# The order of dV and dK at the start of an attention backward pass

## The chip, the cores and the metric

The kernel runs on one core of one Trainium2 chip. The metric is the time of one execution on the device in microseconds (us). The kernel before took 1716.59 us, the median of 3 runs (1715.66 to 1716.76). The profile was taken from one execution whose span was 1714.6 us.

## The reference

One transformer block is computed for one decode step, and then the gradients of everything that goes in. There are 4 sequences, one token each, model width 512, 32 heads of 128, and a cache of 4096 keys and values per sequence and head, all in bf16. The part that matters here is attention:

```python
q = (x @ wq).reshape(B, Sq, H, Dh).transpose(0, 2, 1, 3)
scores = jnp.einsum("bhqd,bhkd->bhqk", q, k_cache) * (Dh ** -0.5)
p = _softmax(scores, axis=-1)
o = jnp.einsum("bhqk,bhkd->bhqd", p, v_cache)
```

A gated MLP follows. The outputs are the block's output and the gradients for x, both caches and all five weights. The gradients of the caches are the large ones. With 4 x 32 = 128 pairs of sequence and head (called heads from here on), each cache is 128 pieces of 4096 x 128 values, 1 MB each. With one query per head, both gradients are outer products: dV of a head is the column p (4096 values) times the row dO (128 values), and dK is the column dS times the row q. dO is the gradient of the attention output, and dS = p (dP - c) times the scale, with dP = V dO and c the sum of dO times O for the head. So dV needs only p and dO, while dK needs dP, for which all of V of that head has to be read again.

## The kernel before, in words

**Forward.** A loop over pairs of heads reads K and V of each head from memory once, computes scores, softmax and output, and keeps p of all heads on chip (`P_all`, 128 x 128 x 32). Then the MLP runs forward and backward, which ends with the gradient `dhT` at the output projection.

**Backward.** V of every head is read a second time, and 128 pieces of dV and 128 pieces of dK are written. For each head s:

- `load_V2` reads V of the head, issued by ACT (nine heads are read by SP ahead of the backward part). Seven slots form a ring for these loads.
- `front(s)` transposes V on TensorE in four groups of eight (`V_T`, line 764), ACT copies each group back from PSUM (line 765), and eight matmuls with the stationary `zd` (line 1178) add dP of the head into a PSUM tile that four heads share. `zd` is written by GpSimd (`dO_window`, line 1143).
- `group_dS(g)` makes dS of four heads at once on VectorE (lines 1192, 1195), after the shared dP tile was copied by ACT and transposed by TensorE.
- `grad_V(s)` and `grad_K(s)` each run one `outer` on VectorE (line 770), which writes 128 x 4096 values into a slot. dV is then stored from GpSimd's queue (line 781), dK from SP's queue (line 1202). For dV, GpSimd first writes p twice side by side (`P_pairs`, line 1148).
- `replicate(i0)` spreads rows of dO and of q over all partitions for four heads: four matmuls into the one PSUM bank of the pool `psrep`, and one copy by ACT, for `rdo` and then for `rq`. Two buffers each, used in turn.

**Order.** The order of instructions is written by hand: each engine runs its instructions in the order in which the Python code issues them, and an engine waits when something that its next instruction needs is not there. So a GpSimd copy stands behind every store that GpSimd issues before it. The loop over heads runs `front` five heads ahead of `grad_K` (L = 5) and `grad_V` three heads ahead (LV = 3):

```python
for s in range(NH):
    load_ahead(s + L)
    if s % REP == 0 and s + REP < NH:
        replicate(s + REP)
    P_pairs(s + L)
    if s + L < NH:
        front(s + L)
    ...
    if s > 0 and s + LV < NH:
        grad_V(s + LV)
    grad_K(s)
```

Ahead of it five heads of `front` are run, with dV of heads 2 and 3. dV of heads 0 and 1 comes earlier still, at the end of the MLP part, from rows of dO made there.

**Slots.** 23 slots of a little over 1 MB hold what is read and written. A list `free` is used first in, first out: `Slot(...)` takes the first, `give()` puts a slot at the end. A slot is given back in the code as soon as the store from it has been issued. Whoever takes it next waits until that store has landed. Slots of the output weights come free page by page, those of the first two V heads go to `free` too. Slots of dV of heads 0 and 1 are held back in `first_gv` and given back only after `front(0)` and `front(1)`.

**Side work.** In the loop `step("o")` prepares dO of later heads from step 2 on (one unit per head), and `step("s")` makes the gradients of the weights and of x from step 21 on: one unit per head, three from head 59.

Of the kernel before, what the change touches and what calls it, by code (L numbers as in the profile page):

```python
# [9 lines left out]
FP32 = mybir.dt.float32  # L10
# [14 lines left out]
def kernel(  # L25
# [22 lines left out]
    nc = tc.nc  # L48
    P = nc.NUM_PARTITIONS
# [5 lines left out]
    Dh = A_k_cache.shape[3]  # L55
    F = B_w1.shape[1]
    NH = B * H
# [105 lines left out]
    ident_b = const.tile([P, P], BF16, name="ident_b")  # L163
# [14 lines left out]
    def ones_window(col):  # L178
# [11 lines left out]
                          in_=rowg[:, None, :, None].to_broadcast([P, 4, 8, 4]))  # L190
# [70 lines left out]
    with ExitStack() as c0:  # L261
# [19 lines left out]
        for r in range(2):  # L281
            for t_ in range(2):
                for q in range(4):
                    nc.tensor.matmul(qr_ps[32 * q:32 * (q + 1), 2 * r + t_, :], lhsT=ident_b[:, 64 * r + t_:64 * (r + 1):2],
                                     rhs=qT_bf[:], start=True, stop=True, tile_position=(0, 32 * q))
# [314 lines left out]
    def step(k, n=1):  # L600
        for _ in range(n):
            next(units[k], None)
# [114 lines left out]
    dOrows_bf = pers2.tile([NH, Dh], BF16, name="dOrows_bf")  # L717
# [4 lines left out]
    qrows_bf = pers2.tile([NH, Dh], BF16, name="qrows_bf")  # L722
# [29 lines left out]
    REP = B  # L752
    reps = {}
# [10 lines left out]
                nc.tensor.transpose(pt[:, i, :], v[:, g * GW + i, :], ident_b[:])  # L764
            nc.scalar.copy(out=v[:, g * GW:(g + 1) * GW, :], in_=pt[:])  # L765

    P2s, first_gv = {}, []

    def outer(dst, col2, row):
        nc.vector.tensor_tensor(  # L770
            out=dst.rearrange("p j (r t) -> p j r t", t=2),
            in0=col2[:, :, None, :].to_broadcast([P, SJ, Dh // 2, 2]),
            in1=row.rearrange("p (r t) -> p r t", t=2)[:, None, :, :].to_broadcast([P, SJ, Dh // 2, 2]),
            op=ALU.mult,
        )

    def grad_V(s):
        b, h = bh_of(s)
        gv = Slot("gv")
        outer(gv.heads(), P2s.pop(s), reps["rdo", s // REP][:, s % REP, :])  # L780
        nc.gpsimd.dma_start(out=rows_of(out_3[b, h]), in_=gv.heads())  # L781
        if s > 1:
            gv.give()
        else:
            first_gv.append(gv)

# [6 lines left out]
    def load_V2(eng=nc.sync):  # L793
        s = nv["next"]
        if s < NH:
            V2s[s] = Slot("V2", vring if vring else free)
            eng.dma_start(out=V2s[s].heads(), in_=cache_head(A_v_cache, s))
            nv["next"] += 1

    with ExitStack() as cm:  # L800
# [33 lines left out]
        for wi, wt in enumerate((w1, w3)):  # L834
            for fc in range(FC):
                for cc in range(DC):
                    nc.tensor.matmul(gu_ps[:, wi, fc, :], lhsT=w13_view(wt, cc)[:, fc * P:(fc + 1) * P], rhs=hhatT[:, cc, :],
                                     start=(cc == 0), stop=(cc == DC - 1))
# [25 lines left out]
        for jj in range(DC):  # L864
            i_mm = 0
            for (lt, wt) in ((d_gateT_bf, w1), (d_upT_bf, w3)):
                for fc in range(FC):
                    nc.tensor.matmul(dn_ps[:, jj, :], lhsT=w13_view(wt, jj)[:, fc * P:(fc + 1) * P], rhs=lt[:, fc, :],
                                     start=(i_mm == 0), stop=(i_mm == 2 * FC - 1))
                    i_mm += 1  # L870
        for sl in w1 + w3:
            sl.give()
        rs = Slot("reps")
        rep_bufs = {nm_: [rs.b()[:, (2 * k + i) * 512:(2 * k + i + 1) * 512].rearrange("p (i d) -> p i d", i=REP) for i in range(2)]
                    for k, nm_ in enumerate(("rq", "rdo"))}
# [4 lines left out]
        ps = psA.tile([P, REP, Dh], FP32, tag="rT", name="repq_ps")  # L880
# [4 lines left out]
        for s in range(3):  # L885
# [8 lines left out]
                         start=True, stop=True)  # L894
# [32 lines left out]
    with ExitStack() as c2:  # L927
        psT = c2.enter_context(tc.tile_pool(name="psT2", bufs=2, space=bass.MemoryType.PSUM))
        psD = c2.enter_context(tc.tile_pool(name="psD", bufs=1, space=bass.MemoryType.PSUM))
        psrep = c2.enter_context(tc.tile_pool(name="psrep", bufs=1, space=bass.MemoryType.PSUM))  # L930
# [176 lines left out]
        def rest_of_dO():  # L1107
            for pg in range(1, H // 8):
                while wo_units and wo_units[0] < 4 * (pg + 1):
                    woT_unit(psT, wo_units.popleft(), "s")  # L1110
                    yield
                dO_columns(8 * pg, 8 * pg + 8, psg, "gps")
                yield
                dO_rows(8 * pg, 8 * pg + 8, psg, "gps")
                mid_w["wo"][pg].give()
                yield
            dr_ps = psg.tile([B, D], FP32, tag="gps", name="dr_ps")
            for c in range(DC):
                nc.tensor.transpose(dr_ps[:, c * P:(c + 1) * P], dhT_f[:, c, :], ident_f[:])
            nc.scalar.copy(out=dh, in_=dr_ps[:])  # L1120

        units["o"] = rest_of_dO()
        def replicate(i0):
            K_ = 8 * B if i0 < 8 * B else P
            for nm_, rows in (("rdo", dOrows_bf), ("rq", qrows_bf)):
                if (nm_, i0 // REP) in reps:
                    continue
                ps = psrep.tile([P, REP, Dh], FP32, tag="rep", name="rep_ps")
                for i in range(REP):
                    nc.tensor.matmul(ps[:, i, :], lhsT=ident_b[0:K_, i0 + i:i0 + i + 1].to_broadcast([K_, P]), rhs=rows[0:K_, :],  # L1130
                                     start=True, stop=True)
                rt = rep_bufs[nm_][i0 // REP % 2]
                nc.scalar.copy(out=rt, in_=ps[:])  # L1133
                reps[nm_, i0 // REP] = rt

        rows = {}
        dS2s = {}
# [7 lines left out]
        def P_pairs(s):  # L1145
            if s < NH and s not in P2s:
                P2s[s] = bw3.tile([P, SJ, 2], BF16, tag="P2", name="P2")
                nc.gpsimd.tensor_copy(out=P2s[s][:], in_=P_all[:, s, :, None].to_broadcast([P, SJ, 2]))  # L1148
# [13 lines left out]
        def front(s):  # L1162
            hl = s % B
            if s not in VTs:
                for g in range(SJ // GW):
                    V_T(s, psT, range(g, g + 1))
                    if hl == 0 and g == 0:
                        rows_out()
                    if hl == 0 and g == 2:
                        rows_T()  # L1170
            VT = VTs[s].heads()
            if hl == 0:
                rows["acc"] = psD.tile([P, 512], FP32, tag="dP", name="dP_ps")
            dO_window(s)
            for u in range(2):
                for c in range(4):
                    j0 = 8 * c + 4 * u
                    nc.tensor.matmul(rows["acc"][32 * c:32 * (c + 1), :], lhsT=zq_window(zd[hl], 2 * hl + u),  # L1178
                                     rhs=VT[:, j0:j0 + 4, :], start=(hl == 0 and u == 0),
                                     stop=(hl == B - 1 and u == 1), tile_position=(0, 32 * c))  # L1180
            if hl == B - 1:
                rows["ps"] = rows.pop("acc")
            sl = VTs.pop(s)
            (vring if len(V2s) + len(VTs) + len(vring) < NV2 else free).append(sl.i)

        def group_dS(g):
            i0 = g * B
            T = rows.pop("T").rearrange("p jj (c m) -> p c m jj", c=4)
            t = rows.pop("t")[:, 0:B * SJ].rearrange("p (b j) -> p b j", b=B)
            t5 = t.rearrange("p b (c u jj) -> p b c u jj", c=4, u=2)  # L1190
            for hl in range(B):
                nc.vector.tensor_scalar(out=t5[:, hl], in0=T[:, :, 2 * hl:2 * hl + 2, :], scalar1=c_rep[:, i0 + hl:i0 + hl + 1],  # L1192
                                        scalar2=scale, op0=ALU.subtract, op1=ALU.mult)
            dS2s[g] = bw3.tile([P, B, SJ, 2], BF16, tag="dS2", name="dS2", bufs=1)
            nc.vector.tensor_tensor(out=dS2s[g][:], in0=t[:, :, :, None].to_broadcast([P, B, SJ, 2]),
                                    in1=P_all[:, i0:i0 + B, :, None].to_broadcast([P, B, SJ, 2]), op=ALU.mult)
# [10 lines left out]
                load_V2(nc.scalar)  # L1207


        O0, S0, L, LV = 2, 21, 5, 3  # L1210

        def load_ahead(s):
            prefetch()
            if s < NH and s not in V2s and s not in VTs:
                load_V2(nc.scalar)

        for s in range(L):
            load_ahead(s)
            P_pairs(s)
            front(s)  # L1220
            if s < 2:
                first_gv[s].give()
            elif s < LV + 1:
                grad_V(s)
        group_dS(0)
        for s in range(NH):
            load_ahead(s + L)
            if s % REP == 0 and s + REP < NH:
                replicate(s + REP)
            P_pairs(s + L)  # L1230
            if s + L < NH:
                front(s + L)
            elif s + L == NH:
                rows_out()
                rows_T()
            if s > 0 and s + LV < NH:
                grad_V(s + LV)
            grad_K(s)
            if s % B == B - 1 and s + 1 < NH:
                group_dS((s + 1) // B)  # L1240
            if s >= S0:
                step("s", 1 if s < S0 + 38 else 3)
            elif s >= O0:
                step("o")
# [31 lines left out]
```

## Time and profile before

| | busy us | share of the span | instructions |
|---|---|---|---|
| TensorE, matmul (PE) | 1271.0 | 74% | 16180 |
| TensorE, weight load (PEld) | 944.0 | 55% | 16180 |
| VectorE (DVE) | 1228.3 | 72% | 1293 |
| ScalarE (ACT) | 969.3 | 57% | 1502 |
| GpSimd (POOL) | 472.3 | 28% | 823 |
| DMA, mean rate | 413 GB/s | | 101740 packets, 707.49 MB |

The page cuts the span into 40 slices of about 43 us, with one digit per engine and slice for its busy share in tenths and the rate of the transfers below. The forward part fills slices 1 to 16, the backward part begins in slice 17. Rows by windows give the same for stretches of any length. A timeline lists the instructions of one engine in order of time: start, duration, engine, line, operation, what it writes and reads, how often; in square brackets the idle time of the engine just before, and what ended it. The costs of single operations in the backward part:

| operation | times | mean ns |
|---|---|---|
| `outer` of dV or dK, DVE | 256 | 2290 |
| copy of eight transposed tiles, ACT | 512 | 1024 |
| dP matmul, PE | 1024 | 453 |
| copy of rep rows, ACT | 62 | 587 |
| P copied in pairs, POOL | 127 | 1056 |
| `zd` written, POOL | 128 | 729 |

The median time from issue to landing is 28.1 us for a store of dV, 19.5 us for a store of dK and 15.6 us for a load of V.

### The profile page before, as it was taken

Reading aid. Unit: us, or ns where it says so; the run is one execution under the profiler, and the core shown is the slowest. Engines: PE = TensorE matmul, PEld = TensorE weight load, DVE = VectorE, ACT = ScalarE, POOL = GpSimd, SP = SyncE. Lnnn points to the kernel's source line nnn. Section 1 sums busy time; section 2 is a strip of 40 time slices with the busy share of each in tenths; the row PEclk is TensorE's granted clock in tenths of the full one; section 3 lists DMA queues with packets and bytes.
Section 4 is the critical chain, followed back from the end, with each engine's and each line's share of the span. In section 5 each row is a group of like instructions: output and inputs, shape, how many; then the busy total and the mean of one; then the engine's idle time right before and its main releaser. Section 6 shows DMA issues by size and latency. Waiting matters only on the chain. (4 is left out here: it accounts for less than half of the span.)

```text
span 1714.6 us, 38302 instructions
## 1 busy us (share of the span) xinstructions
PE 1271.0 (74%) x16180; PEld 944.0 (55%) x16180; DVE 1228.3 (72%) x1293; ACT 969.3 (57%) x1502; POOL 472.3 (28%) x823
## 2 busy tenths in 40 slices
PE   5889888888888888777667777774666776877760
PEld 4767776676666667554445455553454544454440
DVE  5989899989998996466666667663557456565484
ACT  3555444544544454676665655553656775776761
POOL 1211232222222221132231323132335133323250
PEclk9999999999999999998888886876878786677886
DMA  9999999999999999799999999999999999999998
GB/s 400 424 424 424 425 423 424 424 423 422 420 423 411 419 408 399 296 407 425 424 424 423 424 423 424 423 425 424 390 383 372 425 425 421 422 423 423 424 424 337
DMA packets 101740, 707.49 MB, mean 413 GB/s; under 512 B 11052, under 2 KB 15288, under 8 KB 17600
## 3 DMA queue, kind: packets, MB, share of 16 engines
q1 hardware_dynamic: 63568, 432.04, 60.5%
q0 software_dynamic: 20864, 148.22, 20.6%
q10 hardware_dynamic: 17136, 124.79, 17.7%
q8 instruction: 127, 2.08, 0.5%
q14 instruction: 45, 0.37, 0.1%
HBM read 422.59 MB, written 282.34 MB: 411 GB/s over the span
## 5 line engine op out<-in xcount | busy, mean ns | idle before, releaser
L765 ACT COPY V<-pt_tps 128x1024 bf16<-128x1024 bf16 x512 | 491.4, 1024 | 194.9 <-PE pt_tps L764 126.8
L764 PE MATMUL pt_tps<-ident_b,V 128*128 128x128 bf16 x4096 | 370.7, 254 | 144.5 <-ACT V L765 138.9
L764 PEld LDWEIGHTS <-V 128*128 128x128 bf16 x4096 | 320.1, 117 | 214.5 <-issue 206.0
L770 DVE TENSOR_TENSOR gk<-dS,reps 128x4096 bf16<-128x4096 bf16 x128 | 292.6, 2287 | 111.1 <-DMA out_dram<-gv 98.2
L770 DVE TENSOR_TENSOR gv<-P,reps 128x4096 bf16<-128x4096 bf16 x125 | 286.8, 2294 | 117.3 <-DMA out_dram<-gv 106.3
L421 DVE TENSOR_TENSOR PK<-Kn,PK 128x4096 bf16<-128x4096 bf16 x128 | 292.3, 2283 | 26.3 <-POOL PK L417 25.8
L436 PE MATMUL M_ps<-PK,Vn 128*128 128x130 bf16 x4096 | 285.1, 222 | 32.9 <-DMA Vn<-in_A_v_cache_dram 32.2
L436 PEld LDWEIGHTS <-Vn 128*128 128x128 bf16 x4096 | 252.8, 99 | 53.1 <-DMA Vn<-in_A_v_cache_dram 45.8
L328 DVE STREAM_TRANSPOSE KT<-Kn 128x512 f32<-128x512 f32 (+1 forms) x321 | 250.6, 797 | 0.3 <-issue 0.2
L1178 PE MATMUL dP_ps<-V,zd 128*32 128x512 bf16 x1024 | 180.4, 453 | 83.7 <-ACT V L765 61.7
L323 ACT COPY KT<-pt_tps 128x1024 bf16<-128x1024 bf16 x128 | 129.5, 1012 | 184.4 <-PE pt_tps L322 147.1
L781 POOL DMA_DIRECT2D out_dram<-gv x128 | 68.2, 533 | 547.8 <-DVE gv L770 525.0
L417 POOL COPY PK<-P_all 128x64 bf16<-128x64 bf16 x128 | 32.6, 255 | 414.4 <-ACT P_all L411 411.4
L334 POOL TENSOR_TENSOR W<-qrep,wmask 128x128 bf16<-128x128 bf16 x128 | 123.9, 968 | 82.4 <-PE S_ps L354 67.4
L1148 POOL COPY P<-P_all 128x64 bf16<-128x64 bf16 x127 | 134.1, 1056 | 0.0
L1178 PEld LDWEIGHTS <-zd 128*32 128x32 bf16 x1024 | 36.5, 96 | 169.9 <-issue 136.3
L1192 DVE TENSOR_SCALAR dPr<-dPT_ps,c_rep 128x32 f32<-128x32 f32 x128 | 23.1, 242 | 128.4 <-PE dPT_ps L1160 128.2
L1143 POOL COPY zd<-dOT_bf 128x2 bf16<-128x2 bf16 x128 | 93.3, 729 | 3.0 <-PE dP_ps L1178 3.0
L411 ACT COPY P_all<-pt_P 32x64 bf16<-32x64 bf16 x256 | 52.1, 203 | 53.5 <-PE pt_P L407 51.2
L322 PE MATMUL pt_tps<-ident_b,Kn 128*128 128x128 bf16 x1024 | 80.5, 223 | 0.0
L446 PE MATMUL kP_ps<-PK,onesw 128*32 128x512 bf16 x1024 | 79.2, 386 | 0.0
L1133 ACT CAST reps<-rep_ps 128x512 bf16<-128x512 f32 x62 | 36.4, 587 | 71.9 <-PE rep_ps L1130 36.3
(244 smaller groups left out, 1365.7 us busy)
## 6 DMA issues: line engine op xcount, KB each, us to landing
Kn<-in_A_k_cache_dram SPq DMA_DIRECT2D x128, 1024.0 KB, 15.3
Vn<-in_A_v_cache_dram SPq DMA_DIRECT2D x128, 1024.0 KB, 15.7
out_dram<-gv POOLq DMA_DIRECT2D x128, 1024.0 KB, 28.1
out_dram<-gk SPq DMA_DIRECT2D x128, 1024.0 KB, 19.5
V<-in_A_v_cache_dram ACTq DMA_DIRECT2D x119, 1024.0 KB, 15.6
V<-in_A_v_cache_dram SPq DMA_DIRECT2D x9, 1024.0 KB, 18.6
wq<-in_A_wq_dram SPq DMA_DIRECT2D x8, 1024.0 KB, 19.1
out_dram<-gw POOLq DMA_DIRECT2D x6, 896.0 KB, 27.8
```

Source lines behind the costliest of these rows:

```text
L322: nc.tensor.transpose(pt[:, i, :], Kn[:, c * GW + i, :], ident_b[:])
L323: nc.scalar.copy(out=KT[:, c * GW:(c + 1) * GW, :], in_=pt[:])
L328: nc.vector.transpose(out=KT[:, c * w_:(c + n) * w_], in_=Kn[:, c * w_:(c + n) * w_])
L334: nc.gpsimd.tensor_tensor(out=W[:, hl], in0=qrep[:, :, s:s + 1].to_broadcast([P, 4, 32]), in1=wmask[:, hl, None, :].to_broadcast([P, 4, 32 ...
L421: nc.vector.tensor_tensor(out=PK[:, :, 0:Dh].rearrange("p j (r t) -> p j r t", t=2), in0=Ks[s].heads().rearrange("p j (r t) -> p j r t", t=2),
L436: nc.tensor.matmul(hold["M"][:], lhsT=Vn[:, j, :], rhs=PK[:, j, :], start=(j == 0), stop=(j == SJ - 1))
L764: nc.tensor.transpose(pt[:, i, :], v[:, g * GW + i, :], ident_b[:])
L765: nc.scalar.copy(out=v[:, g * GW:(g + 1) * GW, :], in_=pt[:])
L770: nc.vector.tensor_tensor(out=dst.rearrange("p j (r t) -> p j r t", t=2), in0=col2[:, :, None, :].to_broadcast([P, SJ, Dh // 2, 2]), in1=r ...
L1143: nc.gpsimd.tensor_copy(out=zd[s % B][:, 32:132:67], in_=dOT_bf[:, s:s + 1].to_broadcast([P, 2]))
L1148: nc.gpsimd.tensor_copy(out=P2s[s][:], in_=P_all[:, s, :, None].to_broadcast([P, SJ, 2]))
L1178: nc.tensor.matmul(rows["acc"][32 * c:32 * (c + 1), :], lhsT=zq_window(zd[hl], 2 * hl + u), rhs=VT[:, j0:j0 + 4, :], start=(hl == 0 and u ...
```

## The change

dV runs ahead of dK by more heads at the start: in the lead-in, dV of heads 2 to 7 is run (two heads after each of the first three `front` calls), so that eight heads of dV are done before the first dK. The lead stays at eight and shrinks by one every four steps from step 16 on, down to three. It is meant to give the DMA engines something to store while the first dS is made. For that, dO rows and q rows are replicated on their own schedules: `rdo` two heads before dV needs it, `rq` two heads before dK needs it. `P_pairs` moves into the new function `more_V`, behind the dV that it follows. The list `first_gv` goes: the slots of dV of heads 0 and 1 are given back at once.

```diff
-    P2s, first_gv = {}, []
+    P2s = {}
...
         nc.gpsimd.dma_start(out=rows_of(out_3[b, h]), in_=gv.heads())
-        if s > 1:
-            gv.give()
-        else:
-            first_gv.append(gv)
+        gv.give()
...
-        def replicate(i0):
+        def replicate(nm_, i0):
+            if i0 >= NH or (nm_, i0 // REP) in reps:
+                return
...
-        O0, S0, L, LV = 2, 21, 5, 3
+        O0, S0, L = 2, 21, 5
+        gvd = {"n": 2}
+
+        def more_V(upto):
+            while gvd["n"] < min(NH, upto):
+                s = gvd["n"]
+                P_pairs(s)
+                replicate("rdo", s - s % REP)
+                grad_V(s)
+                P_pairs(s + 1)
+                P_pairs(s + 2)
+                gvd["n"] += 1
+                if s % REP == 2:
+                    replicate("rdo", s + 2)
+
+        def lead_V(s):
+            return 8 - min(5, max(0, s - 12) // 4)
...
+        replicate("rdo", REP)
         for s in range(L):
             load_ahead(s)
-            P_pairs(s)
             front(s)
-            if s < 2:
-                first_gv[s].give()
-            elif s < LV + 1:
-                grad_V(s)
+            more_V(min(2 * s + 4, 8))
         group_dS(0)
         for s in range(NH):
             load_ahead(s + L)
-            if s % REP == 0 and s + REP < NH:
-                replicate(s + REP)
-            P_pairs(s + L)
+            if s % REP == 2:
+                replicate("rq", s + 2)
             if s + L < NH:
                 front(s + L)
...
-            if s > 0 and s + LV < NH:
-                grad_V(s + LV)
+            if s > 0:
+                more_V(s + 1 + lead_V(s))
             grad_K(s)
```

More of the change, by code (lines that the diff above doesn't have):

```diff
@@ L1122 @@
         units["o"] = rest_of_dO()
-        def replicate(i0):
+        def replicate(nm_, i0):
+            if i0 >= NH or (nm_, i0 // REP) in reps:
+                return
             K_ = 8 * B if i0 < 8 * B else P
[L1125 to L1134, printed above, removed]
+            rows = dOrows_bf if nm_ == "rdo" else qrows_bf
+            ps = psrep.tile([P, REP, Dh], FP32, tag="rep", name="rep_ps")
+            for i in range(REP):
+                nc.tensor.matmul(ps[:, i, :], lhsT=ident_b[0:K_, i0 + i:i0 + i + 1].to_broadcast([K_, P]), rhs=rows[0:K_, :],
+                                 start=True, stop=True)
+            rt = rep_bufs[nm_][i0 // REP % 2]
+            nc.scalar.copy(out=rt, in_=ps[:])
+            reps[nm_, i0 // REP] = rt
         rows = {}
```

## The prediction

> **What bounds the kernel now.** I read the page's slices first, then the same stretch cut finer, then each engine's timeline there. On the page, the DMA engines are full almost everywhere:
>
> ```profile
> DMA  9999999999999999799999999999999999999998
> GB/s 400 424 424 424 425 423 424 424 423 422 420 423 411 419 408 399 296 407 425 424 424 423 424 423 424 423 425 424 390 383 372 425 425 421 422 423 423 424 424 337
> ```
>
> The kernel is bound by transfers at about 424 GB/s, so a 1 MB head (1,049 kB) costs 1,049/424 = 2.47 us, and time is won only where the rate falls. It falls in slice 17 (296), in slices 29 to 31 (390, 383, 372), and at the two ends. The change acts first on slice 17, where the backward part begins. The answer by windows of 5 and 10 us (busy us of PE, weight load, DVE, ACT, POOL; then granted clock, DMA share, GB/s):
>
> ```profile
> 700.00:705.00 5.00, 1.28 (x15) 0.88 (x12) 3.38 (x5) 2.07 (x3) 2.02 (x8) 1.00 0.86 357
> 705.00:710.00 5.00, 4.18 (x42) 2.96 (x43) 2.32 (x2) 2.59 (x3) 1.49 (x8) 0.66 0.53 220
> 710.00:715.00 5.00, 3.45 (x42) 2.12 (x43) 2.27 (x1) 3.72 (x5) 1.40 (x7) 1.00 0.82 333
> 715.00:720.00 5.00, 3.50 (x43) 2.17 (x43) 0.00 (x0) 3.77 (x5) 0.19 (x1) 1.00 0.57 210
> 720.00:725.00 5.00, 3.50 (x39) 2.17 (x38) 0.22 (x2) 3.72 (x6) 0.00 (x0) 1.00 0.59 211
> 725.00:730.00 5.00, 3.68 (x39) 2.37 (x39) 4.71 (x7) 3.38 (x5) 0.00 (x0) 0.92 0.46 147
> 730.00:740.00 10.00, 7.71 (x84) 5.11 (x82) 7.54 (x4) 7.35 (x9) 5.09 (x6) 0.87 0.97 379
> 740.00:750.00 10.00, 6.74 (x78) 4.26 (x75) 5.64 (x7) 8.71 (x10) 2.13 (x3) 1.00 1.01 425
> ```
>
> Against 424 these rows lack (67+204+91+214+213+277) x 5 + 45 x 10 = 5,780 kB between 700 and 740, or 13.6 us. DVE is idle there while PE and ACT prepare dK. The timeline of DVE says why:
>
> ```profile
> 698.50 2.29 DVE L770 TENSOR_TENSOR gv<-reps 128x4096 bf16<-128x4096 bf16 x1
> 701.03 2.28 DVE L770 TENSOR_TENSOR gv<-reps 128x4096 bf16<-128x4096 bf16 x1
> 706.58 2.29 DVE L770 TENSOR_TENSOR gv<-reps 128x4096 bf16<-128x4096 bf16 x1 [3.16 <-PE dP_ps L1178]
> 709.98 2.29 DVE L770 TENSOR_TENSOR gv<-P,reps 128x4096 bf16<-128x4096 bf16 x1 [1.10 <-POOL P L1148]
> 724.78 0.73 DVE L1192 TENSOR_SCALAR dPr<-dPT_ps,c_rep 128x32 f32<-128x32 f32 x4 [12.51 <-PE dPT_ps L1160]
> 726.00 2.29 DVE L770 TENSOR_TENSOR gk<-dS,reps 128x4096 bf16<-128x4096 bf16 x1
> ```
>
> Four dV heads, then 12.5 us of nothing, until five `front` calls, 5.0 us each, have given the first dS. The timelines of POOL and PE show what is queued behind the first stores:
>
> ```profile
> 701.09 0.63 POOL L781 DMA_DIRECT2D out_dram<-gv  x1 [3.82 <-DVE dOT_bf L739]
> 703.62 0.54 POOL L781 DMA_DIRECT2D out_dram<-gv  x1 [1.90 <-DVE c_rep L749]
> 705.06 0.20 POOL L1143 COPY zd<-dOT_bf 128x2 bf16<-128x2 bf16 x1
> 731.62 1.48 POOL L1148 COPY P<-P_all 128x64 bf16<-128x64 bf16 x1
> 733.04 2.26 POOL L1143 COPY zd<-dOT_bf 128x2 bf16<-128x2 bf16 x1
> ```
>
> ```profile
> 705.32 1.05 PE L1178 MATMUL dP_ps<-V,zd 128*32 128x512 bf16 x8 [3.68 <-POOL zd L1143]
> ```
>
> POOL issues the dV stores and also writes `zd`, without which PE can't do dP and, in order behind it, the transposes of the next head. The `zd` copy takes 0.20 us at 705 but 2.26 us at 733, where DVE runs an `outer` from 732.92 to 735.24.
>
> **What the Trainium skill says.** "SBUF — State Buffer", section "SBUF: two separate sides": DVE and GpSimd share a port pair under an exclusive lock, held for a whole instruction, and a DVE operation with two SBUF inputs takes it against a GpSimd operation that reads SBUF. The trace agrees (0.20 us against 2.26). The same section warns that a DVE operation in a two-port mode also keeps GpSimd from writing DMA descriptors. For this operation the trace does not show it: the store issued at 701.09 moved bytes from 702.0 on while DVE ran until 703.3. "DMA: Bandwidth & Descriptors", section "Anatomy of one DMA — SWDGE (gpsimd) path": about 2.0 us plus bytes/436e3 us, so 4.4 us for a head; the lone store issued at 709.17 landed in 4.4 us.
>
> **The change part by part.** *dV of heads 4 to 7 moves ahead of dK.* Nothing is added to DVE's or the DMA's total work: four heads of 2.29 us and 2.47 us move into the hole. If all fitted without disturbing anything, 4 x 2.47 = 9.9 us of the 13.6 would be filled.
>
> *The slot of head 0 is returned at once.* In the built program gv(0) and gv(1) now take the same slot (before, `first_gv` held slot 11 and gv(1) took slot 0). So gv(1) waits for the first store to land. It landed 5.5 us after 701.09, that is 706.6; with no second store beside it, say 706.0. gv(1) then runs 706.0 to 708.3 instead of 701.03 to 703.3. Behind it on POOL stand its store (708.6), the cast of dOT_f, the four memsets and the first `zd`. gv(2), which now has a free slot, starts at 708.5 and holds the port till 710.8, so memsets and `zd` follow at about 711.7. Behind `zd` waits PE's dP of head 0: 711.8 instead of 705.3, **6.5 us later**, and every `front` after it.
>
> *POOL's order.* After the change `zd` of head 1 stands behind the store of gv(3), and gv(3) waits for the store of gv(1): 708.6 + 4.4 = 713.0, so it runs to 715.3. The P copy ahead of `zd` then waits for gv(4) (to 717.6) and `zd` for gv(5) (to 719.9). PE would have been ready at about 716.6, so 3.3 us more are lost; the later `zd` copies come about as PE needs them. The extra rep copy in the lead-in costs 0.4 + 0.6 us. Sum for the first dS: 6.5 + 3.3 + 0.4, **10.2 us**; the first gk starts at about 736 instead of 726.
>
> *The transfers with these times.* By 740: what moved by 709 without gv(1) (1,785 + 1,098 - 1,049 = 1,834 kB), seven dV heads (7,340), the V loads of heads 9 and 10 (2,097) and 1.6 us of the next two (680): 11,950 kB = 28.2 us of 40, so 11.8 us lost against 13.6: 1.8 us won. One bound more: in the kernel before, the first gk and the V load beside it ran slowly (82, 213, 336, 221, 262 GB/s from 728 to 733, or 2.4 us lost). If that restart is as slow after the change, the gain is 1.8 - 2.4 = -0.6. I take +1.0, with both ends kept.
>
> *The lead shrinking from 8 to 3 at heads 16 to 32.* Five steps have no dV. The 20 steps hold 55 transfers instead of 60: 6.8 us a step against 7.4. `front` and a wo transpose came every 5.3 to 6.4 us (the V loads of ACT at 739.27, 744.84, 751.24), so compute still keeps up: cost nothing, hidden behind the transfers. At the end the lead is 3 as before, so the tail is unchanged.
>
> *rq and rdo replicated apart, earlier.* The same 62 copies. ACT's waits for a gk still reading the buffer (20.2 us, 7 times) and PE's for the one rep bank (35.2 us, 31 times) should go. From 730 to 1200 the DMA is full, so nothing is gained there. From 1200 to 1340 the rate fell to 385, 391, 425, 353, 405, 351, 387 in windows of 20 us, 12.8 us lost, where PE, ACT and DVE in turn run late. Four groups of heads there, perhaps 0.6 us each (the gap between the two copies is 0.5 to 0.7 us): 0 to 2.5 us, taken as 1.0. Those holes start from waits for wq and for old gk stores, which the change leaves.
>
> Sum: -1.0 - 1.0 = -2.0 us, 1714.6.
>
> **The rivals.** *The holding on POOL is milder* (copies slip in between DVE operations; dP of head 1 at 716.6): the first dS is only some 7 us late, 3.3 us more are won, the restart is overlapped by waiting dV stores and the later holes shrink by 2: 1.8 + 3.3 + 2 = 7, so 1709.5. For it: gv(5) and gv(6) each wait for a landing, which leaves DVE gaps. Against: 733.04. *The wait of gv(1) is harmless*: all 9.9 us, 1706.7. For it: the hole is wide. Against: PE stood 3.68 us for that very `zd`. *The new waits are worse*: a P copy at 1310.13 took 8.10 us under back-to-back `outer` operations. If that hits a `zd` in the lead-in, dK starts some 15 us late and V loads, issued by ACT behind each `front`, with it: 5 more us of DMA idle, less the 1 to 2 won: 1720, slower.
>
> **How the numbers follow.** Near-cancellation 0.53, milder 0.26, full gain 0.08, worse 0.13. So 1714.6; faster by over 3.4 us 0.34, within 0.53, slower 0.13. The range leaves out the full gain (0.08) and about half of the worst case: 1709.0 to 1719.0.
>
> **What would show it.** On DVE, gv(1) starting near 706 with a wait for a gv store; `zd` of head 0 near 711.7; eight gv before the first gk, which starts near 736; the rate from 700 to 740 still under 424 by about 12 us' worth; no ACT wait for gk at the rep copies. I am wrong if gv(1) starts near 701, if the first gk stays near 726 to 730, or if the holes from 1200 to 1340 change by several us.

## The result, and the profile after

The changed kernel took 1714.35 us (median of 4 runs, 1713.38 to 1718.53); the kernel before, beside it, 1716.13 us (1715.66 to 1716.76). The ratio is 0.9994, with a 95% interval of 0.9977 to 1.0011: no difference that this measurement can tell. A second measurement with more runs, told below, gave 1.0001 (0.9992 to 1.0010). Single executions of one kernel lie several us apart (13 of the changed kernel in the second measurement took 1712.39 to 1720.62 us), so spans of single profiles are not compared here to the microsecond; places within a profile are.

The profile of the changed kernel comes from an execution whose span was 1716.7 us. In it the backward part began 1.0 us later than in the profile of before (first dV, gv(0), at 699.52 us instead of 698.50), so I give moments in the lead-in as distance from gv(0). The slices of the page first:

```profile
DMA  9999999999999999799999999999999999999997
GB/s 402 424 425 424 424 423 425 424 424 424 414 423 409 420 406 399 318 397 425 424 426 425 412 424 425 426 426 425 420 365 381 421 421 408 419 422 425 423 424 312
```

Slice 17, at which the change was aimed, has 318 GB/s instead of 296, and slice 18 has 397 instead of 407. The hole is still there. A small dip is new in slice 23 (412). The same stretch by windows (busy us of PE, weight load, DVE, ACT, POOL; then granted clock, DMA share, GB/s):

```profile
700.00:705.00 5.00, 3.07 (x59) 2.57 (x56) 2.11 (x3) 3.13 (x5) 0.63 (x1) 0.84 0.91 378
705.00:710.00 5.00, 0.00 (x0) 0.00 (x0) 2.90 (x3) 0.00 (x0) 0.31 (x1) 0.50 0.14 61
710.00:715.00 5.00, 2.46 (x23) 1.62 (x24) 2.12 (x2) 0.37 (x1) 3.37 (x10) 0.50 0.81 341
715.00:720.00 5.00, 2.98 (x30) 2.06 (x29) 4.87 (x3) 3.49 (x4) 2.77 (x5) 0.74 0.57 238
720.00:725.00 5.00, 2.99 (x40) 1.98 (x39) 4.74 (x3) 3.76 (x4) 4.72 (x6) 0.94 0.96 390
725.00:730.00 5.00, 4.45 (x43) 3.17 (x40) 1.33 (x1) 3.63 (x5) 2.68 (x7) 0.72 1.00 351
730.00:740.00 10.00, 7.00 (x84) 4.57 (x83) 5.62 (x8) 7.49 (x9) 0.00 (x0) 1.00 0.98 337
740.00:750.00 10.00, 6.96 (x82) 4.30 (x81) 6.66 (x4) 7.67 (x10) 4.17 (x5) 1.00 1.00 390
```

From 720 to 730 the transfers now run at 390 and 351 GB/s, where before they ran at 211 and 147. But from 705 to 710 PE and ACT do nothing at all and the rate is 61 GB/s. From 725 to 740 the DMA share is 0.98 to 1.00 while only 337 to 351 GB/s move. The timeline of DVE:

```profile
699.52 2.29 DVE L770 TENSOR_TENSOR gv<-reps 128x4096 bf16<-128x4096 bf16 x1
707.10 2.29 DVE L770 TENSOR_TENSOR gv<-reps 128x4096 bf16<-128x4096 bf16 x1 [4.96 <-DMA out_dram<-gv]
709.41 2.28 DVE L770 TENSOR_TENSOR gv<-reps 128x4096 bf16<-128x4096 bf16 x1
714.57 11.76 DVE L770 TENSOR_TENSOR gv<-P,reps 128x4096 bf16<-128x4096 bf16 x5 [2.88 <-DMA out_dram<-gv]
734.31 0.73 DVE L1189 TENSOR_SCALAR dPr<-dPT_ps,c_rep 128x32 f32<-128x32 f32 x4 [7.98 <-PE dPT_ps L1157]
735.53 2.29 DVE L770 TENSOR_TENSOR gk<-dS,reps 128x4096 bf16<-128x4096 bf16 x1
```

Eight heads of dV stand before the first dK, as written. gv(1) waits 4.96 us for the landing of the first dV store. The idle time ahead of the first dS is 7.98 us instead of 12.51, but the first gk comes 36.0 us after gv(0) instead of 27.5. The timelines of POOL and of PE's dP show the chain between:

```profile
709.69 0.54 POOL L781 DMA_DIRECT2D out_dram<-gv  x1 [6.95 <-DVE c_rep L749]
712.30 0.19 POOL L1140 COPY zd<-dOT_bf 128x2 bf16<-128x2 bf16 x1
...
717.16 0.53 POOL L781 DMA_DIRECT2D out_dram<-gv  x1 [3.80 <-DVE gv L770]
717.69 1.47 POOL L1145 COPY P<-P_all 128x64 bf16<-128x64 bf16 x1
719.10 0.19 POOL L1140 COPY zd<-dOT_bf 128x2 bf16<-128x2 bf16 x1
```

```profile
712.54 1.04 PE L1175 MATMUL dP_ps<-V,zd 128*32 128x512 bf16 x8 [8.30 <-POOL zd L1140]
719.35 0.61 PE L1175 MATMUL dP_ps<-V,zd 128*32 128x512 bf16 x8 [1.73 <-POOL zd L1140]
724.19 1.24 PE L1175 MATMUL dP_ps<-V,zd 128*32 128x512 bf16 x8 [1.00 <-POOL zd L1140]
```

PE stands 8.30 + 1.73 + 1.00 = 11.03 us for `zd` in the lead-in, where before it stood 3.68 us once. A second profile of the same kernel has 9.59 + 1.70 + 0.28 = 11.57 us; in it gv(1) comes 8.3 us and the first gk 36.1 us after gv(0).

To compare whole runs I worked out, from windows of 20 us, how many us of full transfer each stage lacks: the sum of (424 - rate) x 20 / 424. A small negative value means that the stage ran at 425 to 426. The stages begin at the same moment in every profile; moving the first one by the 1.0 us by which the changed kernel is late gives 12.0 for it instead of 12.1.

| kernel (one profile each) | 700-760 us | 760-1180 | 1180-1360 |
|---|---|---|---|
| before | 13.5 | 0.1 | 12.8 |
| changed | 12.1 | 0.0 | 11.0 |
| changed, second profile | 12.1 | 3.7 | 3.6 |
| changed, slots of gv(0), gv(1) held back | 11.7 | -0.2 | 10.6 |
| changed, `zd` ahead of the stores | 10.8 | 2.5 | 10.0 |
| changed, both | 6.8 | 1.0 | 10.0 |
| changed, slots held, `zd` of four heads up front | 7.3 and 7.1 | 0.7 and 0.8 | 9.0 and 7.9 |
| the same, `zd` early in the loop too | 7.1 | 0.8 | 7.6 |
| changed, lead stays 8 | 12.5 | -1.6 | 8.9 |
| changed, slots held, `zd` of four heads up front, lead stays 8 | 7.2 | -1.1 | 10.0 |
| changed, lead shrinks 28 steps later | 12.0 | 5.0 | 5.5 |
| changed, lead shrinks in five steps on end | 12.2 | -1.6 | 13.7 |
| before, with rq and rdo replicated apart | 14.7 | -1.0 | 10.3 |

The first column is steady: five profiles with the changed lead-in give 12.0 to 12.5. The two other columns are not: the two profiles of the changed kernel itself have 0.0 and 11.0, and 3.7 and 3.6. So a difference of a few us there, between single profiles, says little about a kernel.

### The profile page after: what moved, and what is told of

Same layout as the page of the kernel before. It is cut to its first block, busy times and chain, and to the rows that moved or that the text cites. A ratio compares the mean times of both kernels' runs of the same rounds, so it can differ in the third digit from the quotient of the medians.

```text
span 1716.7 us, 38321 instructions
## 1 busy us (share of the span) xinstructions
PE 1252.2 (73%) x16180; PEld 930.7 (54%) x16180; DVE 1228.7 (72%) x1293; ACT 967.6 (56%) x1502; POOL 523.7 (31%) x821
## 5 line engine op out<-in xcount | busy, mean ns | idle before, releaser
L764 PE MATMUL pt_tps<-ident_b,V 128*128 128x128 bf16 x4096 | 361.4, 250 | 168.2 <-ACT V L765 162.2
L764 PEld LDWEIGHTS <-V 128*128 128x128 bf16 x4096 | 310.6, 114 | 232.4 <-issue 224.0
L1175 PE MATMUL dP_ps<-V,zd 128*32 128x512 bf16 x1024 | 172.6, 453 | 111.7 <-ACT V L765 55.9
L1145 POOL COPY P<-P_all 128x64 bf16<-128x64 bf16 x125 | 151.7, 1214 | 0.0
L1140 POOL COPY zd<-dOT_bf 128x2 bf16<-128x2 bf16 x128 | 130.3, 1022 | 0.0
L1130 ACT CAST reps<-rep_ps 128x512 bf16<-128x512 f32 x62 | 36.4, 587 | 98.4 <-PE rep_ps L1127 59.6
L411 ACT COPY P_all<-pt_P 32x64 bf16<-32x64 bf16 x256 | 52.1, 203 | 53.9 <-PE pt_P L407 51.6
## 6 DMA issues: line engine op xcount, KB each, us to landing
V<-in_A_v_cache_dram ACTq DMA_DIRECT2D x119, 1024.0 KB, 13.5
```

What stands on the lines that cost most here:

```text
L1140: nc.gpsimd.tensor_copy(out=zd[s % B][:, 32:132:67], in_=dOT_bf[:, s:s + 1].to_broadcast([P, 2]))
```

## The experiments

Each group of runs shares its runs of the kernel before, on the same chip; kernels of different groups are compared by their ratios. Medians are in us; the ratio is to the kernel before, with its 95% interval.

### The changed kernel once more

Edit: none.

> The changed kernel once more, beside the others of this set. Theory (near-cancellation): -2 us against the kernel before, 1713 to 1715.5; gv(1) starts about 5 us after the first dV store with a wait for it, first dK near 735, and 700 to 740 us lacks about 12 us' worth of transfers. Rival (the first profile of it, 1718.5, was the typical case): 1716 or more.

1714.91 beside 1714.85 (43 runs of before), ratio 1.0001 (0.9992 to 1.0010). The change as a whole is worth nothing within 0.1%. This is the value that the next experiments are read against.

### The slots of gv(0) and gv(1) held back again

```diff
-        gv.give()
+        if s > 1:
+            gv.give()
+        else:
+            first_gv.append(gv)
...
             front(s)
+            if s < 2:
+                first_gv[s].give()
             more_V(min(2 * s + 4, 8))
```

> The changed kernel, with the slots of dV of heads 0 and 1 held back again until front(0) and front(1), as before the change. Theory (the early return of the slot makes gv(1) wait for a landing, and everything behind it on GpSimd and TensorE moves 6.5 us): gv(1) back at about 701, the first zd at about 705, the first dK at about 730 to 732 (zd of heads 1 to 3 still stand behind the stores), 700 to 740 lacks about 7 us' worth instead of 12 to 14, and the time falls by 4 to 6 us against the changed kernel: about 1709.5. Rival (the slot wait is hidden, since the dV stores that follow fill the DMA anyway): first dK within 1 us, the same time within 1.5 us.

1713.37, ratio 0.9989 (0.9983 to 0.9996). gv(1) again starts 2.5 us after gv(0), and the first dP comes 6.7 us after gv(0) instead of 13.0. Yet the first gk comes 35.0 us after gv(0), 1.0 us sooner. PE's dP in this kernel, by the timeline:

```profile
706.81 1.04 PE L1178 MATMUL dP_ps<-V,zd 128*32 128x512 bf16 x8 [1.85 <-POOL zd L1143]
715.01 1.04 PE L1178 MATMUL dP_ps<-V,zd 128*32 128x512 bf16 x8 [3.40 <-POOL zd L1143]
723.69 1.04 PE L1178 MATMUL dP_ps<-V,zd 128*32 128x512 bf16 x8 [4.00 <-POOL zd L1143]
```

The wait of 8.30 us shrinks to 1.85, and those of the next heads grow from 1.73 and 1.00 to 3.40 and 4.00: 9.25 us in all against 11.03. The wait for the slot is real, but behind it stands the next one, `zd` behind dV stores on GpSimd.

### `zd` of the next head written before the dV stores

```diff
         def dO_window(s):
+            if s >= NH or s in zds:
+                return
+            zds.add(s)
...
             front(s)
+            dO_window(s + 1)
             more_V(min(2 * s + 4, 8))
```

> The changed kernel, with zd of the next head written by GpSimd right after each front call of the lead-in, ahead of the two dV stores, instead of behind them. Theory (zd of heads 1 to 3 behind the stores costs TensorE about 3 to 4 us): no wait of the dP matmuls for zd of heads 1 to 3, the first dK about 3 to 4 us earlier than in the changed kernel, the time 1 to 3 us lower, about 1712.5. Rival (this delay is hidden behind the dV stores that are moving at that time): first dK earlier, but the time within 1 us of the changed kernel.

1715.04, ratio 1.0004 (0.9996 to 1.0012). The later waits of PE for `zd` in the lead-in are gone, but the first, 8.47 us, stays, and the first gk comes 34.4 us after gv(0). In the first column 1.3 us is won, and nothing of it is seen in the time.

### Both repairs

Edit: the two diffs above together.

> Both at once: the slots of dV of heads 0 and 1 held back, and zd of the next head ahead of the stores. Theory: the two delays add, so the first dK starts at about 726 to 728, nearly as in the kernel before, the four dV heads fill 8 to 10 of the 13.6 us, 700 to 740 lacks 4 to 5 us' worth, and the time is 7 to 9 us below the changed kernel's start, about 1707. Rival (the hole is kept open by V loads, which can't start earlier than front frees their slots): no better than holding the slots alone, 1709.5 to 1711. Second rival (later holes between 1200 and 1340 grow by what is won at the start): the first dK early, the time still 1713 or more.

1710.07, ratio 0.9971 (0.9960 to 0.9982): 4.8 us under the changed kernel, where the single repairs gave 1.5 and nothing. The first gk comes 30.2 us after gv(0), and PE now stands 1.94 us for the first `zd` and 2.58 us for that of head 3:

```profile
705.11 1.04 PE L1183 MATMUL dP_ps<-V,zd 128*32 128x512 bf16 x8 [1.94 <-POOL zd L1148]
723.00 1.05 PE L1183 MATMUL dP_ps<-V,zd 128*32 128x512 bf16 x8 [2.58 <-POOL zd L1148]
```

The hole holds 6.8 us instead of 12.1; these 5.3 us fit the 4.8 us of time. The two waits cover each other: whichever is taken away alone, the other ends only a little earlier. By the times alone this is near the edge of the intervals; the hole says it clearly, with 0.4 and 1.3 us won by the single repairs and 5.3 by both. That the two delays would simply add, and give 1707, was a wrong expectation.

### `zd` of four heads up front, twice

The slots of gv(0) and gv(1) are held back here as above; `zd` of heads 0 to 3 is written ahead of the lead-in, later ones two heads ahead in it. The kernel was measured in two groups.

```diff
+        for s in range(B):
+            dO_window(s)
         for s in range(L):
             load_ahead(s)
             front(s)
+            dO_window(s + 2)
+            if s < 2:
+                first_gv[s].give()
             more_V(min(2 * s + 4, 8))
```

> The kernel that holds the first two slots, with zd of all four first heads written before any later dV store, and in the lead-in two heads ahead. Theory (zd behind stores is what still delays front(3) by 2.6 us when zd is one head ahead): no wait of the first 20 dP groups for zd, the first dK 2 to 3 us earlier against the first dV than with zd one ahead (about 27.5 us after it, as in the kernel before), 700 to 760 lacks 5 us' worth or less, the time about 1 to 2 us below the kernel with zd one ahead: 1708 to 1709. Rival (by then the DMA has dV to move and the earlier front is hidden): first dK earlier, the loss from 700 to 760 and the time as with zd one ahead, 1710.

1707.91 beside 1714.61, ratio 0.9965 (0.9952 to 0.9977). Its second measurement:

> The kernel with both repairs of the lead-in and the lead shrinking as in the changed kernel, once more beside the one that keeps lead 8. Theory A: ratio 0.9965 as before, so 2 to 4 us slower than the one with lead 8. Theory B: the same time as the one with lead 8.

1708.42 beside 1714.97, ratio 0.9962 (0.9950 to 0.9974). The timeline of DVE in this second profile:

```profile
698.39 2.29 DVE L770 TENSOR_TENSOR gv<-reps 128x4096 bf16<-128x4096 bf16 x1
700.92 2.28 DVE L770 TENSOR_TENSOR gv<-reps 128x4096 bf16<-128x4096 bf16 x1
...
717.96 6.92 DVE L770 TENSOR_TENSOR gv<-P,reps 128x4096 bf16<-128x4096 bf16 x3 [2.41 <-DMA out_dram<-gv]
725.13 0.73 DVE L1197 TENSOR_SCALAR dPr<-dPT_ps,c_rep 128x32 f32<-128x32 f32 x4 [0.26 <-PE dPT_ps L1165]
725.90 0.45 DVE L1200 TENSOR_TENSOR dS<-dPr,P_all 128x256 bf16<-128x256 f32 x1
726.38 2.29 DVE L770 TENSOR_TENSOR gk<-dS,reps 128x4096 bf16<-128x4096 bf16 x1
```

DVE now goes from dV to the first dS with 0.26 us of idle time, and the first gk comes 28.0 us after gv(0), nearly as soon as in the kernel before (27.5), with eight heads of dV ahead of it instead of four. The windows of the same profile, in the same columns as above:

```profile
705.00:710.00 5.00, 4.66 (x42) 3.25 (x43) 2.58 (x2) 2.67 (x3) 1.28 (x6) 0.58 0.50 210
710.00:715.00 5.00, 3.19 (x42) 2.09 (x40) 3.75 (x2) 3.72 (x5) 0.78 (x2) 1.00 0.86 351
715.00:720.00 5.00, 3.50 (x42) 2.17 (x42) 2.59 (x2) 4.00 (x6) 0.77 (x2) 1.00 0.81 306
720.00:725.00 5.00, 3.76 (x43) 2.34 (x41) 4.75 (x3) 3.72 (x5) 4.36 (x5) 1.00 1.00 393
725.00:730.00 5.00, 3.51 (x41) 2.16 (x40) 4.80 (x7) 3.77 (x5) 1.22 (x4) 1.00 0.97 303
730.00:740.00 10.00, 7.00 (x82) 4.35 (x82) 3.17 (x2) 7.67 (x10) 1.67 (x5) 1.00 1.01 425
```

This is the most that dV ahead of dK brought in these runs: the stage lacks 7.1 us instead of 13.5, which is 6.4 us, and the time is 6.55 us under that of before. Against the kernel with the two simple repairs the further gain (0.9962 and 0.9965 against 0.9971) is within the intervals.

### `zd` early in the loop too

```diff
             if s + L < NH:
                 front(s + L)
+                dO_window(s + L + 2)
```

(on top of the kernel of the last section)

> As the previous one, and zd written two heads ahead in the whole loop, ahead of the dV store of each step. Theory (in the changed kernel TensorE waits for zd 45 times, 115 us in all, against 18 times, 45 us, before; part of it lies where TensorE is late, from 1180 to 1360): those waits mostly gone, the loss from 1180 to 1360 lower by 1 to 4 us, and the time lower by as much: about 1706 to 1707. Rival (these waits lie where the DMA is full): the waits gone, the time the same within 1 us.

1709.46 beside 1714.61, ratio 0.9970 (0.9960 to 0.9980): no gain. The waits of this kernel (us in total, times, longest) show what came instead:

```profile
POOL zd L1148 <- PE dP_ps L1183: 121.2, 31, 11.8
```

Written two heads early, `zd` waits for PE to finish with its buffer, and GpSimd's stores stand behind that. PE's own waits for `zd` are gone all the same: 2.0 us in all, where the kernel of the last section has 41.9. So taking them away brought no time. Whether that is because the transfers are full there, or because the new waits of GpSimd took the gain back, these runs don't separate.

### rq and rdo replicated apart, alone

```diff
-        def replicate(i0):
+        def replicate(nm_, i0):
...
-            if s % REP == 0 and s + REP < NH:
-                replicate(s + REP)
+            if s % REP == 2:
+                replicate("rq", s + 2)
...
             if s > 0 and s + LV < NH:
                 grad_V(s + LV)
+                if (s + LV) % REP == 2:
+                    replicate("rdo", s + LV + 2)
```

(on the kernel before, the lead left at 3; dV of the lead-in replicates `rdo` in the same way)

> The kernel before, with dO and q rows replicated on their own schedules, two heads ahead, and nothing else of the change (the lead of dV stays three, first_gv stays). Theory (the earlier replication relieves TensorE and ScalarE a little where they are late): the time 0 to 2.5 us below the kernel before, 1713.5 or so; ScalarE's waits for a dK still reading the rep buffer (20 us in the kernel before) nearly gone. Rival (those waits only move to another instruction of the same engine): the total idle time of ScalarE and the time unchanged within 1 us.

1715.97 beside 1714.61, ratio 1.0009 (1.0001 to 1.0018): a loss of about 1.4 us, only just clear of the noise, where I had taken a gain of 1.0. The waits of ScalarE at these copies in the kernel before, which is new here:

```profile
ACT reps L1133 <- PE rep_ps L1130: 36.3, 42, 4.0
ACT reps L1133 <- DVE gk L770: 20.2, 7, 5.0
```

and in this one:

```profile
ACT reps L1133 <- PE rep_ps L1130: 62.3, 53, 3.8
```

The wait for a gk that still reads the buffer is gone, as forecast. What I hadn't seen is that ScalarE now waits 26 us more for the matmuls that feed the copy, and that PE waits for `zd` longer too, 52.1 us in all instead of 21.6. So a longer wait for `zd`, which the changed kernel shows as well (55.4), can come with the replication alone. The loss in time shows neither at 1180 to 1360 (10.3 us lacking against 12.8) nor at 760 to 1180; 1.2 us of it stand in the lead-in (14.7 against 13.5). One profile each can't settle more.

### The lead stays 8

```diff
         def lead_V(s):
-            return 8 - min(5, max(0, s - 12) // 4)
+            return 8
```

> The changed kernel, with the lead of dV kept at eight heads to the end instead of shrinking to three from step 16 to 32. Theory (the shrinking costs nothing): the time within 1 us of the changed kernel, no transfers lost between 760 and 1180 us in either. Rival (while the lead shrinks, five steps without dV leave the DMA short: 396 GB/s from 960 to 980 in the first profile of the changed kernel, and 407 to 402 around 920 in two other runs): that loss of 1 to 4 us gone and the time lower by as much; at the end more dK than dV are left, and the last stores come no later.

1710.77 beside 1714.61, ratio 0.9978 (0.9969 to 0.9988): by the ratios about 4 us under the changed kernel (1.0001), which was not in this group; so shrinking is not free there. I looked for the cause in the trace. In the second profile of the changed kernel ScalarE stands still three times for 3.9 to 10.2 us between 915 and 1011 us; the first two times look as follows (ACTq is its queue of DMA issues):

```profile
923.86 0.34 ACTq L794 DMA_DIRECT2D V<-in_A_v_cache_dram  x1
924.29 0.59 ACT L1130 CAST reps<-rep_ps 128x512 bf16<-128x512 f32 x1 [3.87 <-DMA out_dram<-gk]
...
952.82 0.33 ACTq L794 DMA_DIRECT2D V<-in_A_v_cache_dram  x1
953.25 0.59 ACT L1130 CAST reps<-rep_ps 128x512 bf16<-128x512 f32 x1 [4.91 <-DMA out_dram<-gk]
```

The third, 10.15 us, ends at 1010.97. The copy didn't wait for anything of its own: the V load ahead of it in ScalarE's order was issued only at 923.86 and 952.82, each time when a dK store had landed. Counted from the start, they are the loads of heads 37 and 41, and the third is that of head 49. In the built program the V loads and the dK stores take turns at eight completion signals (counters that a transfer raises when it has landed), and ahead of each V load stands a wait until the transfer before it at its signal has landed. For these three loads that transfer is the dK store of head 23, 27 and 35. With lead 8, as in the kernel before, no load of heads 35 to 71 follows a dK store at its signal, and no such wait stands from 900 to 1060 us. Two more kernels try whether that is the price of shrinking.

### The lead shrinks later

```diff
-            return 8 - min(5, max(0, s - 12) // 4)
+            return 8 - min(5, max(0, s - 40) // 4)
```

> The changed kernel with its lead shrinking from 8 to 3 at steps 44 to 60 instead of 16 to 32. Theory A: shrinking costs because steps without a dV leave one store out while the step takes as long, so the same loss appears later: dips in the DMA rate about 200 us later than the 930 to 1030 us of the changed kernel, time unchanged, ratio about 1.000. Theory B: what costs is the pairing of particular V loads with dK stores at steps 23 to 35, which moves when the steps move; the pairs now fall at heads 56, 57, 65 and 69, so a loss could move there too; no loss at all would speak for the place, not for the shrinking. Ratio 0.998 if nothing is lost.

1714.81 beside 1714.97, ratio 1.0001 (0.9993 to 1.0009). The dips went along, as the first theory had it, and the deepest came at one of the heads that the second had named. Windows and ScalarE's timeline of this kernel:

```profile
900.00:940.00 40.00, 29.87 (x300) 20.76 (x300) 25.95 (x22) 24.34 (x28) 7.71 (x19) 0.88 1.01 426
1140.00:1150.00 10.00, 8.87 (x63) 6.27 (x62) 1.90 (x6) 6.00 (x7) 0.00 (x0) 0.51 0.76 306
1150.00:1160.00 10.00, 7.54 (x91) 5.47 (x87) 10.00 (x5) 6.36 (x7) 5.71 (x5) 1.00 0.85 299
```

```profile
1136.69 0.33 ACTq L794 DMA_DIRECT2D V<-in_A_v_cache_dram  x1
1137.12 0.59 ACT L1130 CAST reps<-rep_ps 128x512 bf16<-128x512 f32 x1 [13.04 <-DMA out_dram<-gk]
```

The load issued at 1136.69 is that of head 65, which shares its signal with dK of head 51. ScalarE stood 13 us for it, PE and DVE had next to nothing to do meanwhile (1.33 and 0.00 us busy from 1130 to 1140), and then the rate fell to about 300 GB/s for 20 us, 5.7 us lost. Not every such wait is as dear: two of 12.07 and 10.93 us, which end at 1061.72 and 1076.69, are followed by 408 GB/s in one window of 20 us, 0.8 us lost.

### The lead shrinks at once

```diff
-            return 8 - min(5, max(0, s - 12) // 4)
+            return 8 - min(5, max(0, s - 12))
```

> The changed kernel with its lead going from 8 to 3 in five steps on end, 13 to 17, instead of one step in four. Theory A (steps without a dV store starve the transfers): the five steps without dV stand together, the backlog of stores runs dry, and the dip is deeper: 5 steps with one store of 2.47 us each missing, less what dK hastens, 3 to 10 us more than the changed kernel, ratio 1.002 to 1.006. Theory B (V loads that wait for the landing of a dK store): with this spacing no V load of heads 35 to 71 follows a dK store in its row of completion signals, so ScalarE shows no wait for a dK landing at 900 to 1060 us, and the time is that of lead 8 kept to the end, ratio 0.998.

1713.72 beside 1714.97, ratio 0.9991 (0.9983 to 0.9999). Five steps on end without a dV store starve nothing: no window of 20 us from 760 to 1220 is under 420 GB/s. ScalarE has no wait for a dK landing from 900 to 1060. So steps without dV are not by themselves the cause of the dips there. The V loads that wait for a dK store are what is left, and the other profiles bear that out. Eight of them (the kernels with the lead-in of the change, repaired or not, that shrink at steps 16 to 32) have 12.2 to 21.5 us of these waits between 900 and 1060, and seven of these have a window of 20 us there at 389 to 409 GB/s; in the eighth (`zd` early in the loop, 12.9 us) the lowest is 422. None of the six without such waits is under 422.

But the waits don't settle the time. The repaired lead-in that shrinks has them as long as the changed kernel has, and is no slower than the one with lead 8 of the next section; ScalarE's waits for dK landings at the rep copies from 900 to 1060, first of the changed kernel, then of the repaired one:

```profile
ACT reps L1130 <- DMA out_dram<-gk: 18.9, 3, 10.2
ACT reps L1133 <- DMA out_dram<-gk: 17.8, 3, 10.2
```

Nor is the time of this kernel clearly that of lead 8 (0.9978, 0.9969 to 0.9988; the intervals overlap a little). Its windows of 1260 to 1320 are together worse than in any other profile of this study:

```profile
1260.00:1280.00 20.00, 16.16 (x173) 12.50 (x173) 8.02 (x9) 13.23 (x16) 4.20 (x3) 0.78 0.76 285
1280.00:1300.00 20.00, 14.20 (x191) 10.26 (x189) 10.87 (x5) 15.63 (x18) 10.39 (x8) 1.00 1.01 420
1300.00:1320.00 20.00, 9.20 (x83) 4.82 (x83) 17.10 (x22) 10.17 (x14) 12.56 (x9) 0.75 0.80 330
```

In this one profile, what wasn't lost at 900 to 1030 was lost there; in the profile of lead 8 it was not (-1.6 and 8.9).

### Both: the repaired lead-in, and the lead stays 8

Edit: the diff of `zd` of four heads up front, with `return 8` in `lead_V`.

> The two repairs of the lead-in (slots of gv(0) and gv(1) held back until front(0) and front(1); zd of heads 0 to 3 written ahead of the lead-in) together with dV eight heads ahead to the end. Theory A: the two losses are independent, one before 740 us and one after 900 us, so their gains add: the lead-in repair alone was worth 6.7 us against before, lead 8 to the end alone about 3.5 us against the changed kernel as it is; the time should be 9 to 10 us under that of before, ratio 0.994 to 0.995. Theory B: both gains are one and the same, the bytes of dV written early instead of late; then the time is that of the repaired lead-in alone, ratio about 0.9965.

1707.85 beside 1714.97, ratio 0.9965 (0.9952 to 0.9978); the kernel whose lead shrinks, beside it, 0.9962. The gains don't add. Once the lead-in is repaired, keeping the lead at 8 brings nothing that can be measured. It does take the waits at 900 to 1060 away (-1.1 us lacking at 760 to 1180 instead of 0.7 and 0.8), and 10.0 us are lacking at 1180 to 1360 instead of 7.9 and 9.0. Why lead 8 brings 4 us with the unrepaired lead-in and none with the repaired one stays open.

The best kernels of the study are these two, at 1708 us: 0.35 to 0.38% under before and as much under the changed kernel.

## Why the prediction was right, and where its steps were not

The time forecast, 1714.6 us as near-cancellation, is what came: 1714.35, and 1714.91 in the longer measurement. Point by point:

- **The slot of gv(0).** Right in mechanism and size. gv(1) 7.5 us after gv(0) was forecast, 7.6 and 8.3 measured in the two profiles; the first dP 13.3 us after gv(0) forecast, 13.0 and 13.7 measured.
- **POOL's order.** Right in mechanism, but oversized: PE's wait for `zd` of head 1 was put at 3.3 us and measured 1.73, because the P copy (717.69, 1.47 us) and `zd` (719.10) passed one right after the other, where I had let each wait for an `outer` of its own. The wait of dP of head 2, 1.00 us, was put at nothing. The first gk was 8.5 us later than before, against 10.2; dP of head 1, 19.8 us after gv(0), came between the forecast (21.4) and its milder rival (18.1). The Trainium skill's "SBUF — State Buffer", section "SBUF: two separate sides", describes the lock, held for a whole instruction; the trace agrees in kind (the P copy at 717.69 took 1.47 us while DVE ran five `outer` operations on end, the one at 727.16 0.25 us while DVE was idle), but a small copy, `zd` at 719.10 with 0.19 us, did get in right behind it.
- **The transfers.** 1.8 us less lost at best and -0.6 at worst, +1.0 taken; 13.5 - 12.1 = 1.4 measured. By 740, 11.8 us were to be lacking; 11.3 were. The lower end rested on a slow restart with the first dK store. The rate is low from 725 to 740, but the first gk ends only at 737.8 and its store comes after that, so most of this stretch is something else.
- **The full gain of 9.9 us.** Named as a rival at 1706.7, and rightly not taken for this kernel. The repaired kernels come to 1708, so it was the two waits, and not the idea, that held it down: 6.4 of the 9.9 us came in the lead-in once they were gone. This is shown by removing them: one alone is worth little, because the other takes its place. Why the last 3 us don't come was not tried.
- **The lead from 8 to 3, "cost nothing, hidden behind the transfers".** Wrong in this kernel. My average of 6.8 us a step against a `front` every 5.6 to 6.4 us (so by the three loads that I named; 5.3 was misread) holds, as the shrinking at once shows, but I looked at rates only. Shrinking moves the order of dK stores against V loads, and by that which load waits for which store. Lead 8 is 4 us faster in this kernel; at 760 to 1180 its profile lacks -1.6 us, the two of the changed kernel 0.0 and 3.7. That these transfers make the time is not shown, since lead 8 brings none in the repaired kernel, where the same waits stand.
- **rq and rdo apart, -1.0.** Wrong in sign. ScalarE's wait for gk went away, and so did PE's for the rep bank (35.2 us before, not among the waits after). ScalarE's wait for the rep matmuls went from 36.3 to 59.6 us, PE's for `zd` from 21.6 to 55.4, and 19.6 us of waits for dK landings stand before these copies. Alone it costs about 0.1%.
- **The holes at 1180 to 1360.** I would be wrong, I wrote, if they changed by several us. In one profile of the changed kernel they did (3.6 us lacking, 12.8 before), in the other hardly (11.0). Two profiles of one kernel lie so far apart that this sign can't decide.

The sum does not close. With the terms as measured it would be 1.4 us won in the lead-in, about 1.4 lost by replicating apart (1.2 of them in the lead-in, where they may be counted already) and about 4 lost by shrinking: 3 to 4 us slower than before. Measured are 0.1 us slower in the longer measurement and 1.8 faster in the first. What makes up for it stays open; the price of shrinking was 4 us in one pair of kernels and nothing in the other. That the total came out as forecast is therefore in part luck: two terms beside the lead-in were wrong, both in the same direction, and either something not on the list stood against them or the prices don't add. The steps of the lead-in, which carry the argument, were right to 2 us each, and the experiments bear out their mechanism.

## What to carry to other kernels

When work is moved ahead to fill a hole, look first at what the filling instructions do to the chain that ends the hole: here the early stores stood ahead of a 0.2 us copy that this chain needed, and the slot of the first was taken back at once. When two waits on one chain cover each other, take them away together; removing one alone looks like a refutation and is none. And an instruction that only issues a load can still stop its engine: find it in the timeline where a compute instruction "waits" for a transfer that it doesn't read.

## What the runs showed of the hardware

- A load waited for stores that have nothing to do with its data, through a completion signal that the program shares between them: 3.87, 4.91 and 10.15 us in the changed kernel and 13.04 us in the one that shrinks later, and ScalarE's compute with it.
- Full DMA share is not full rate: from 725 to 740 us the changed kernel moved 337 to 351 GB/s at a share of 0.98 to 1.00, where most of the run moves 424. In the repaired kernel it was 303 at 0.97 from 725 to 730. Most of it lies before the first dK store, which was issued at 737.85; its cause was not tried.
- The full rate itself differs a little between executions: 424 GB/s over most of the profile of before, 425 to 426 in several others. Over 900 us that comes, by an estimate from these rates, to 2 to 4 us, as large as what some of these edits change.
